# A planned attention and token/channel mixer kernel: all engine orders set anew, last row group in two parts

## The chip, the cores and the metric

The kernel runs on one core of one Trainium2 chip. The metric is device microseconds of one execution. A core has a matmul engine (TensorE, PE in the profile, with its weight loads listed apart as PEld), a vector engine (VectorE, DVE), an activation engine (ScalarE, ACT), a general one (GpSimd, POOL) and a queue engine (SyncE, SP). Each runs its own instructions in the order in which the program lists them, and waits at semaphores for the others. PSUM, where matmuls write, has eight banks.

## The reference

Attention over 4 batches, 8 heads, 768 positions and 64 elements a head, with a mask of blocks (neighbours, first and last rows and columns, and three sampled blocks a row), then a mixer over the 4 x 768 x 512 result:

```python
scores = scale * np.matmul(q, k.transpose(0, 1, 3, 2))      # scale = 1/8
scores = np.where(mask, scores, -1e9)
attn = softmax(scores)                                      # over keys
x = np.matmul(attn, v)             # heads side by side: 4 x 768 x 512
h = np.maximum(xt @ w_tok1, 0.0) @ w_tok2     # xt = x transposed: mixes the 768 positions, 256 hidden
u = x + h.transpose(0, 2, 1)
h2 = np.maximum(u @ w_ch1, 0.0) @ w_ch2       # mixes the 512 channels, 1536 hidden
return u + h2
```

## The kernel before

Two heads make a pair, and there are 16 pairs `p`, four a batch. Each pair has three query tiles `t` of 256, and each of those has three key steps `jj` of 256, so there are 144 steps and 48 units `(p, t)`.

A step is four score matmuls (L917), one exp of 128 x 1024 on ACT (L930) and, in its unit, the product of the probabilities with v (L1086, or L375 for 64-row matmuls). Pairs 0 to 3 (phase 0) carry the mask in 24 extra contraction rows, so their score matmuls have 88 rows. Pairs 4 to 15 (phase 1) use 64-row matmuls, two side by side, and a multiply of the probabilities with a mask on DVE (`cut`, L948), one for the three steps of a unit. `norm` (L1040, L1041) divides by the row sums. K and q are transposed on PE for pairs below 8 (`transposes`, L858 and L823, evacuated at L834, L871 or L887) and by DMA for the others.

When a batch's x is complete, the token mixing follows (`tok_first` for batch 0 pair by pair, `tok_halves` and `tok_full` for the others), then a transpose to `uT`, then the channel mixing `ch`: `uT` with `w_ch1`, relu into `rc`, `rc` with `w_ch2`, an add on DVE (`fin`, L1567 or L1615 and L1622) and the output DMA on SP. The last batch's `ch` has nothing left to mix with. Its last group of 128 rows is written in parts of 256, 128 and 128 columns (L1594).

In `halves` (L365) two 64-row products accumulate in one bank, one pass after the other. Between the passes a no-operation on SP or POOL (`fence`, L358) waits for the first.

The order of every engine is set ahead of time by a planner (`Planner`, L104) that runs while the program is built. It keeps a clock for PE, ACT, DVE and SP and one time `Ev` for each result. An operation has a cost for each engine that may run it, the results it needs, and a priority (the smallest goes first). At each moment a free engine takes the ready operation of the best priority, and its result is dated with the cost, a latency (`lat`) and a semaphore's 50 ns (L283). The order so found is the order in the program; the times are used for nothing else. The priorities and limits are named knobs in `BASE`, overridden by `BY_TIME` for each stretch of planned time (`stretch`). The planner's costs are written beside each operation: `act_cost`, `dve_psum`, 948 for an exp, 1719 for a `cut` over three steps.

Loads are issued on POOL in a fixed order. `landing` dates each as the queue's last landing plus its bytes at 200 B/ns, plus an extra from `LATE` for the first nine, in the order v of pair 0, k, q, v of pair 1, k, q, v of pair 2, and the two token weights.

Of the kernel before, what the change touches and what calls it, by code (L numbers as in the profile page):

```python
# [18 lines left out]
    backp=0.45, backt=0.3, turn=[1], ra=5,  # L19
)  # L20
BY_TIME = {
    0: dict(cch=2),
    1: dict(norm=2.3, m2=300.0, tokp=0.7, ev2=2.0, cch=3),
    2: dict(m2=450.0, ev2=0.9, cpo=1),
    3: dict(norm=2.3, m2=300.0, tokp=0.7, ev2=2.0, cch=3, cpm=3, shift=6000.0, add=0.3, grace=100.0, ev4=1.2),
    5: dict(norm=2.3, m2=150.0, tokp=0.7, ev2=2.0, cch=3, cpm=3, shift=6000.0, add=0.3, grace=100.0, ev4=1.2, cps2=3, relayk=2.0, cut=0.7),
    6: dict(fin=4.1, cps=3, trp=1.6),
    7: dict(fin=4.1, cps=3, trp=1.6),
    8: dict(fin=4.1, cps=3, trp=1.6, add=0.3, back=1.1, cut=0.5),
    9: dict(shift=6000.0),  # L30
    10: dict(fin=4.1, cps=3, trp=1.6, add=0.3, back=1.1, cut=0.5, m2=300.0, ev2=0.9, jit=300.0),
    12: dict(fin=4.1, cps=3, trp=1.6, add=0.3, back=1.1, cut=0.5, m2=300.0, ev2=0.9, jit=300.0, tokp=1.7, backp=0.9, cpo=2, m1=0.0),
    13: dict(fin=4.1, cps=3, trp=1.6, add=0.3, back=1.1, cut=0.5, m2=300.0, ev2=0.9, jit=2000.0, tokp=1.7, backp=0.9, cpo=2, m1=0.0, late=3.5, relayk=0.8),
    14: dict(m2=0.0, cch=2, m1=0.0, cut=6.0, ev4=1.2),
    16: dict(add=0.3, late=1.05, cch=2, ev4=2.0, relayk=3.5),
    17: dict(m1=0.0, back=1.1, add=0.95),
    18: dict(m1=0.0, back=1.1, add=0.95, cut=1.1, m2=300.0, cpo=2),
    19: dict(cps2=3, toks=0.4, jit=300.0, relayv=3.0, relayk=3.5),
    20: dict(m1=0.0, back=1.1, add=0.95, cut=1.1, m2=0.0, cpo=2, toks=-0.5, backp=0.45, cpm=1),
    21: dict(m1=0.0, back=1.1, add=0.95, cut=1.1, m2=0.0, cpo=2, toks=-0.5, backp=0.45, cpm=1),  # L40
    22: dict(m1=100.0, back=1.1, add=0.95, cut=6.0, m2=0.0, cpo=2, toks=-0.5, backp=0.45, cpm=1, relayk=0.8),
    23: dict(m1=100.0, back=1.1, add=0.95, cut=6.0, m2=0.0, cpo=2, toks=-0.5, backp=0.45, cpm=1, relayk=0.8, jit=300.0, cps=3),
    24: dict(m1=100.0, back=1.1, add=0.95, cut=6.0, m2=0.0, cpo=2, toks=-0.5, backp=0.45, cpm=1, relayk=0.8, jit=300.0, cps=3),
    25: dict(jit=450.0, cps2=2, relayv=4.6),
    27: dict(jit=450.0, cps2=2, relayv=4.6, cps=2, backp=0.45, cpo=2, relu=0.85),
    28: dict(jit=450.0, cps2=2, relayv=4.6, cps=2, backp=0.45, cpo=2, relu=0.85),
    29: dict(jit=450.0, cps2=2, relayv=4.6, cps=2, backp=0.45, cpo=2, relu=0.85, toks=0.4, relayk=4.5),
    30: dict(jit=450.0, cps2=2, relayv=4.6, cps=2, backp=0.45, cpo=1, relu=0.85, norm=0.6, cpm=2, backt=0.9),
    31: dict(back=1.1, cpm=1, jit=1300.0),
    32: dict(jit=450.0, cps2=2, relayv=4.6, cps=2, backp=0.45, cpo=1, relu=0.85, norm=1.0, cpm=2, backt=0.9, m1=100.0, shift=0.0),  # L50
    33: dict(tokp=0.7, cps=3, ev4=1.2, shift=-6000.0, cch=2),
    34: dict(chs=0.8, m1=100.0, ev2=1.2, cpo=2, backt=0.2),
    35: dict(jit=0.0, cpo=2, chs=1.1),
}


class Knobs(dict):

    at, by_time, stretch = 0.0, BY_TIME, 5000.0

# [43 lines left out]
class Planner:  # L104
# [108 lines left out]
    def step(self):  # L213
# [36 lines left out]
        for eng in ("act", "dve", "sp"):  # L250
# [3 lines left out]
            best, exp_at = None, 1e18  # L254
# [5 lines left out]
            for o in self.ops:  # L260
# [4 lines left out]
                if eng == "act" and prio > 0 and self.now + cost["act"] > exp_at + KN["grace"]:  # L265
                    continue
# [8 lines left out]
            if best is not None:  # L275
                prio, num, engines, cost, deps, emit, done, lat, tags = chosen
                self.ops.remove(chosen)
                emit(eng)
                c = cost[eng]
                if self.trace is not None:  # L280
                    self.trace.append((self.now, eng, KN[prio] if isinstance(prio, str) else prio, c))
                self.free_at[eng] = self.now + c
                done.t = self.now + c + lat + self.SEM  # L283
                moved = True
# [10 lines left out]
def kernel(  # L295
# [119 lines left out]
    LATE = (0, 0, 600, 200, 400, 0, 0, 1500, 0)  # L415
# [325 lines left out]
    def act_cost(n):  # L741
        return 0.8333 * n + 95.0

    def dve_psum(n, half=1.0):
        return (150.0 + n * half) / 0.96
# [7 lines left out]
    def relayout(p):  # L753
        lays = {}
        for nm in ("k", "q", "v") if p >= NT0 else ("v",):
# [21 lines left out]
            lays[nm + "ev"] = P.op(("dve", "act") if p >= BASE["ra"] else ("dve",), {"dve": 320.0, "act": 735.0}, deps, emit,  # L777
# [5 lines left out]
    def crossbar(p):  # L783

        lays = relayout(p)
        for nm, bufs, there in (("k", ktb, kT_there), ("q", qtb, qT_there)):
# [6 lines left out]
            ev = P.op(("sp",), {"sp": 1300.0}, deps, emit, prio=1, lat=5000.0)  # L793
            there[p, 0], there[p, 1] = ev, ev

    def transposes(p):
# [15 lines left out]
        for nm, bufs, there in (("k", ktb, kT_there), ("q", qtb, qT_there)):  # L812
# [3 lines left out]
            if p >= NT0 and P.phase == 1:  # L816
# [22 lines left out]
                ev = P.op(("dve", "act"), {"dve": 555.0, "act": 740.0}, [last], evac, prio="ev4")  # L839
# [28 lines left out]
            if p >= NT0:  # L868
                def evac(eng, buf=bufs[p % NV], box=box):
# [4 lines left out]
                    ("dve", "act"), {"dve": 555.0, "act": 740.0}, [last], evac, prio="ev4"  # L874
# [5 lines left out]
            for hd in range(2):  # L880
# [8 lines left out]
                ev = P.op(("dve",), {"dve": 550.0}, [last], evac, prio="ev2")  # L889
# [18 lines left out]
    CUTS = (((0,), (1,), (2,)), ((0, 1), (2,)), ((0, 1, 2),), ((0,), (1, 2)))[BASE["cuts"]]  # L908
# [839 lines left out]
```

The softmax here doesn't subtract the row's maximum and nothing guards it: scores larger than these inputs give would overflow.

## Time and profile before

| | us |
|---|---|
| median of 3 runs (lowest, highest) | 245.59 (245.1, 245.77) |
| span of the profiled execution | 243.4 |
| median less span: what lies around it | 2.2 |
| HBM read, written | 26.74 MB, 6.29 MB |
| DMA engines, mean rate over the span | 108 GB/s |

The page gives the time in which each engine was busy, 40 slices of the span, the chain of work that ended last (followed back from the last instruction to what released each one) and the costliest groups of instructions. In a group's line stand the source line, the engine, the operation, what is written and read, the count, the busy time and the mean of one, and after the bar the time for which the engine stood still just before such instructions and what ended that. A windows view gives the busy time of each engine in a stretch, and a timeline the instructions of a stretch in order, neighbours of one kind merged. Ends of matmuls are modelled, starts are recorded. The duration of an ACT or DVE instruction includes some 100 or 80 ns in which the next one already runs: the exp is recorded with 1025 ns, but with work waiting the next begins 921 ns after it.

### The profile page before, as it was taken

How to read it: one execution, taken by the hardware profiler on the slowest of the kernel's cores; microseconds unless marked ns; L12 is line 12 of the kernel's file. 1: busy time of each engine (PE TensorE's matmuls, PEld its weight loads, DVE VectorE, ACT ScalarE, POOL GpSimd, SP SyncE). 2: the span in 40 equal slices, each digit the busy share in tenths (PEclk: the TensorE clock that was granted, in tenths of full speed). 3: DMA queues.
4: the chain of work that ended last, by engine and by line, in shares of the span. 5: the costliest groups of instructions: out<-in, count | busy, mean ns of one | idle time of the engine just before them, and what ended most of it. 6: DMA issues, size and time to landing. Idle time of an engine off the chain costs nothing.

```text
span 243.4 us, 9647 instructions
## 1 busy us (share of the span) xinstructions
PE 237.0 (97%) x4343; PEld 170.9 (70%) x4343; DVE 172.1 (71%) x285; ACT 170.0 (70%) x187; POOL 49.5 (20%) x86
## 2 busy tenths in 40 slices
PE   7999999999999999999999999999999999999994
PEld 3689999767777677867878667677688664565444
DVE  5975987979899889799789788987687535100222
ACT  6889999868797699788778987798658400366000
POOL 8966987357710000000000000000000000000000
PEclk9999999999999999999999999999999999999999
DMA  7999999999993874131207270501030024200132
GB/s 163 166 214 203 209 207 203 206 201 196 201 180 76 132 167 137 38 118 33 40 3 89 46 155 3 154 25 67 3 67 3 5 89 127 112 3 0 43 132 86
DMA packets 39755, 26.17 MB, mean 108 GB/s; under 512 B 21985, under 2 KB 37105, under 8 KB 39713
## 3 DMA queue, kind: packets, MB, share of 16 engines
q0 software_dynamic: 15104, 12.98, 33.9%
q1 hardware_dynamic: 24064, 12.17, 20.4%
q8 instruction: 34, 0.56, 0.9%
q10 hardware_dynamic: 544, 0.39, 0.6%
q14 instruction: 9, 0.07, 0.1%
HBM read 26.74 MB, written 6.29 MB: 136 GB/s over the span
## 4 chain that ended last, share of the span: by engine, by line
PE 89%; DMA 3%; ACT 3%; POOL 2%; DVE 1%; issue 0%; POOLq 0%; DVEq 0%; ACTq 0%
PE banks L375 53%; PE banks L917 14%; PE banks L1601 9%; PE banks L1536 6%; DMA kraw<-in_k_dram 3%; ACT et L930 3%; PE banks L1086 3%; PE banks L858 1%; PE banks L1354 1%; DVE et L948 1%; POOL vraw L447 1%; PE banks L1296 1%; PE banks L1376 1%; PE banks L1318 1%; POOL ktb L517 0%
## 5 line engine op out<-in xcount | busy, mean ns | idle before, releaser
L930 ACT ACTIVATE et<-banks 128x1024 bf16<-128x1024 f32 x144 | 141.6, 1025 | 28.3 <-PE banks L917 24.5
L948 DVE TENSOR_TENSOR et<-et,mask 128x2976 bf16<-128x2976 bf16 x36 | 61.3, 1703 | 8.3 <-ACT et L930 8.2
L917 PE MATMUL banks<-qtb,ktb 64*128 64x256 bf16 (+1 forms) x576 | 63.7, 270 | 0.7 <-ACT et L930 0.2
L375 PE MATMUL banks<-uT,w_ch 64*128 64x512 bf16 (+1 forms) x576 | 60.6, 322 | 0.0
L375 PE MATMUL banks<-w_ch,rc 64*128 64x512 bf16 x384 | 54.3, 376 | 0.0
L375 PEld LDWEIGHTS <-et 64*128 64x128 bf16 x1728 | 39.2, 94 | 9.4 <-POOLq L361 3.0
L917 PEld LDWEIGHTS <-ktb 64*128 64x128 bf16 (+1 forms) x576 | 33.8, 94 | 15.1 <-issue 1.4
L375 PE MATMUL banks<-vaug,et 64*128 64x65 bf16 x1728 | 42.0, 190 | 0.2 <-issue 0.2
L375 PEld LDWEIGHTS <-w_ch 64*128 64x128 bf16 x576 | 28.6, 94 | 8.4 <-SPq L361 0.6
L1128 ACT ACTIVATE rc<-banks 128x512 bf16<-128x512 f32 (+1 forms) x28 | 21.0, 749 | 17.0 <-PE banks L1536 15.0
L1615 DVE TENSOR_TENSOR o<-banks,x 128x512 f32<-128x512 f32 x7 | 4.8, 692 | 28.2 <-PE banks L1601 28.2
L1130 DVE TENSOR_SCALAR rc<-banks 128x1024 bf16<-128x1024 f32 x17 | 20.8, 1221 | 3.4 <-PE banks L375 3.2
L375 PEld LDWEIGHTS <-rc 64*128 64x128 bf16 x384 | 17.3, 94 | 7.9 <-POOLq L361 0.5
L1601 PE MATMUL banks<-w_ch,rc 128*128 128x512 bf16 (+2 forms) x120 | 21.3, 337 | 0.0
L1601 PEld LDWEIGHTS <-rc 128*128 128x128 bf16 x120 | 10.7, 98 | 10.6 <-issue 0.8
L375 PEld LDWEIGHTS <-w_tok 64*128 64x128 bf16 x288 | 14.5, 109 | 3.3 <-POOLq L361 0.6
L1041 DVE TENSOR_TENSOR x<-banks,recip 128x256 bf16<-128x256 f32 x36 | 15.3, 425 | 1.2
L1536 PE MATMUL banks<-uT,w_ch 128*128 128x512 bf16 (+1 forms) x96 | 15.8, 326 | 0.0
L1536 PEld LDWEIGHTS <-w_ch 128*128 128x128 bf16 x96 | 9.4, 98 | 6.4
L1567 DVE TENSOR_TENSOR o<-banks,x 128x1024 f32<-128x1024 f32 x8 | 9.8, 1224 | 5.1 <-PE banks L375 5.0
L1086 PE MATMUL banks<-vaug,et 128*128 128x65 bf16 x288 | 13.1, 193 | 0.0
L1264 DVE TENSOR_TENSOR x<-banks,x 128x512 bf16<-128x512 f32 (+2 forms) x12 | 10.3, 887 | 2.9 <-PE banks L375 2.7
(122 smaller groups left out, 198.0 us busy)
## 6 DMA issues: line engine op xcount, KB each, us to landing
out_dram<-o SPq DMA_DIRECT2D x8, 512.0 KB, 3.6
w_ch<-in_moe_w_ch_dram POOLq DMA_DIRECT2D x8, 384.0 KB, 9.8
vraw<-in_v_dram POOLq DMA_DIRECT2D x10, 192.0 KB, 7.9
out_dram<-o SPq DMA_DIRECT2D x7, 256.0 KB, 2.0
kraw<-in_k_dram POOLq DMA_DIRECT2D x9, 192.0 KB, 9.2
qraw<-in_q_dram POOLq DMA_DIRECT2D x9, 192.0 KB, 8.3
w_tok<-in_moe_w_tok_dram POOLq DMA_DIRECT2D x2, 384.0 KB, 10.0
qf<-in_v_dram POOLq DMA_DIRECT2D x4, 192.0 KB, 7.8
```

The source lines that it names most:

```text
L375: mms.append(nc.tensor.matmul(out=outs()[o](x), lhsT=lhs(o, x, r), rhs=rhs(o, x, r), start=(back == 0 and x == 0), stop=(back == 1 and x = ...
L917: nc.tensor.matmul(out=ps[:, hd, 256 * i : 256 * i + 256], lhsT=ktb[n][rows, h, 256 * jj + 128 * i : 256 * jj + 128 * i + 128], rhs=qtb[n] ...
L930: nc.scalar.activation(out=ets[p, t][:, jj, :, :, :].rearrange("k i h q -> k h i q"), in_=ps.rearrange("k h (i q) -> k h i q", i=2), func= ...
L948: nc.vector.tensor_tensor(out=et, in0=et, in1=free(mask[:, 2 * lo, 256 * t + EDGE : 256 * t + EDGE + 1], 0, [[S, 2 * n], [0, 2], [1, w]]), ...
L1041: nc.vector.tensor_tensor(out=free(xs[b][:, pb // 2, 2 * t, 128 * (pb % 2) : 128 * (pb % 2) + 128], 0, [[64, 2], [256, 2], [1, 64]],), in0 ...
L1086: nc.tensor.matmul(out=po[:, hd, c, :], lhsT=et[:, jj, i, hd, 128 * c : 128 * c + 128], rhs=va[:, hd, 2 * jj + i, 0:65], start=(jj == 0 an ...
L1128: nc.scalar.activation(out=o(), in_=src(), func=AF.Relu)
L1130: nc.vector.tensor_scalar(out=o(), in0=src(), scalar1=0.0, scalar2=None, op0=ALU.max)
L1264: nc.vector.tensor_tensor(out=u, in0=src, in1=u, op=ALU.add)
L1536: nc.tensor.matmul(out=in_bank(pbox["pm"], [k, 128 * n])[:, x // 4, :], lhsT=w_ch1[:, x % 4, 128 * cc : 128 * cc + 128], rhs=st[b]["uT"][: ...
L1567: nc.vector.tensor_tensor(out=t[:, :, :].rearrange("p c (g e) -> p g c e", g=2), in0=free(banks[:, pbox["pm"][0], :], 0, [[256, 2], [512, ...
L1601: nc.tensor.matmul(out=pbox["pm"][:, 0:n], lhsT=box["rc"][:, cc, 128 * sc : 128 * sc + 128], rhs=w_ch2[:, cc, lo : lo + n], start=(cc == 0 ...
```

## The change

The knobs get a value for each 2.5 us of planned time instead of 5; nearly all values are new. The planner's durations, the latency after ACT operations and the extras of the loads are replaced. The mask multiply can be split in a different way for each unit (`cuts=1` is steps 0 and 1 together, then 2; `cuts=0` three single ones; before, `cuts=2` for all). A rule is added by which DVE does not begin an operation of a priority above `urge` that would end later than 200 ns (at `hold=1200`) before one at or below `urge` is ready. Two options, `early` and `part`, are added and are 0. The last row group is written in parts of 384 and 128 columns.

```diff
-    backp=0.45, backt=0.3, turn=[1], ra=5,
+    backp=0.45, backt=0.3, turn=[1], ra=5, early=0, part=0, hold=0.0, urge=-0.5,
...
-BY_TIME = {
-    0: dict(cch=2),
-    1: dict(norm=2.3, m2=300.0, tokp=0.7, ev2=2.0, cch=3),
...
+BY_TIME = {}
+for _lo, _hi, _knobs in (
+    (0, 1, dict(cch=2)),
+    (2, 2, dict(cch=3, ev2=2.0, m2=300.0, norm=2.3, tokp=0.7)),
...
+    (8, 8, dict(backt=0.3, cuts=0, ev4=2, m1=200, relayk=3.5)),
...
+    (18, 19, dict(backt=0.3, cut=1.1, cuts=1, ev4=2, fin=2.1, hold=1200, jit=450, m1=200, m2=450, relayk=3.5, relu=0.85, shift=6000.0)),
...
+    (58, 59, dict(back=1.1, backp=0.45, backt=0.3, cpm=2, cps2=2, cut=1.1, cuts=1, ev2=0.9, ev4=2, fin=2.1, hold=1200, jit=450, m1=200, m2=450, norm=1, relayk=3.5, relayv=4.6, toks=-0.5, urge=0.5)),
...
-    at, by_time, stretch = 0.0, BY_TIME, 5000.0
+    at, by_time, stretch = 0.0, BY_TIME, 2500.0
...
+            if eng == "dve" and KN["hold"] > 0:
+                for o in self.ops:
+                    p = KN[o[0]] if isinstance(o[0], str) else o[0]
+                    if p <= KN["urge"] and "dve" in o[2]:
+                        t = self.when(o[4], o[8])
+                        if t is not None:
+                            soon = min(soon, max(t, self.now))
...
+                if eng == "dve" and prio > KN["urge"] and self.now + cost["dve"] > soon + 1e3 - KN["hold"]:
+                    continue
...
-                done.t = self.now + c + lat + self.SEM
+                done.t = self.now + c + lat + self.SEM + (55.0 if eng == "act" else 0.0)
...
-    LATE = (0, 0, 600, 200, 400, 0, 0, 1500, 0)
+    LATE = (0, 0, 970, 0, 1360, 0, 0, 730, 150)
...
-        return 0.8333 * n + 95.0
+        return 0.8333 * n + 62.0
...
-        return (150.0 + n * half) / 0.96
+        return (100.0 + n * half) / 0.96
...
-                ev = P.op(("dve", "act"), {"dve": 555.0, "act": 740.0}, [last], evac, prio="ev4")
+                ev = P.op(("dve", "act"), {"dve": 500.0, "act": 660.0}, [last], evac, prio="ev4")
...
-    CUTS = (((0,), (1,), (2,)), ((0, 1), (2,)), ((0, 1, 2),), ((0,), (1, 2)))[BASE["cuts"]]
+    CUTS = (((0,), (1,), (2,)), ((0, 1), (2,)), ((0, 1, 2),), ((0,), (1, 2)))
+    cut_of = {}
...
-        exps[jj] = P.op(("act",), {"act": 948.0}, [done], exp, prio=0, lat=80.0)
+        exps[jj] = P.op(("act",), {"act": 915.0}, [done], exp, prio=0)
...
-        for group in CUTS:
+        for group in CUTS[cut_of.setdefault((p, t), KN["cuts"])]:
...
-            ev = P.op(("dve",), {"dve": 158.0 + (537.0 - 4.2 * EDGE) * len(group)},
+            ev = P.op(("dve",), {"dve": 90.0 + 520.0 * len(group)},
...
-            parts[-1:] = [(NC - 1, 0, 256), (NC - 1, 256, 128), (NC - 1, 384, 128)]
+            parts[-1:] = [(NC - 1, 0, 384), (NC - 1, 384, 128)]
...
-                    o = sbw.tile([128, 256], FP32, tag="olast", bufs=3, name=f"o{b}_{sc}_{lo}")
+                    o = sbw.tile([128, 384], FP32, tag="olast", bufs=2, name=f"o{b}_{sc}_{lo}")
...
-                    g, e = lo // 256, lo % 256
-                    nc.vector.tensor_tensor(
-                        out=o[:, 0:n], in0=pbox["pm"][:, 0:n],
-                        in1=st[b]["u"][:, g, sc, e : e + n], op=ALU.add,
-                    )
+                    cuts = sorted({lo, max(lo, min(lo + n, 256)), lo + n})
+                    for l0, l1 in zip(cuts, cuts[1:]):
+                        nc.vector.tensor_tensor(
+                            out=o[:, l0 - lo : l1 - lo], in0=pbox["pm"][:, l0 - lo : l1 - lo],
+                            in1=st[b]["u"][:, l0 // 256, sc, l0 % 256 : l0 % 256 + l1 - l0], op=ALU.add,
+                        )
```

The other operations' planned durations change in the same way (the 768-element copies of a relayout from 320 and 735 to 290 and 660, `norm` from 610 to 570, a DMA transpose's latency from 5000 to 3500 or from 4000 to 3400).

## The prediction

> **What bounds the kernel now.** I read the page's engine shares, slices and chain first, then the windows view stretch by stretch, then the timeline of the stretches where TensorE is not full.
>
> ```profile
> span 243.4 us, 9647 instructions
> ...
> PE 237.0 (97%) x4343; PEld 170.9 (70%) x4343; DVE 172.1 (71%) x285; ACT 170.0 (70%) x187; POOL 49.5 (20%) x86
> ...
> PE   7999999999999999999999999999999999999994
> ...
> PE 89%; DMA 3%; ACT 3%; POOL 2%; DVE 1%; issue 0%; POOLq 0%; DVEq 0%; ACTq 0%
> ...
> L930 ACT ACTIVATE et<-banks 128x1024 bf16<-128x1024 f32 x144 | 141.6, 1025 | 28.3 <-PE banks L917 24.5
> L948 DVE TENSOR_TENSOR et<-et,mask 128x2976 bf16<-128x2976 bf16 x36 | 61.3, 1703 | 8.3 <-ACT et L930 8.2
> ```
>
> The page says TensorE (PE) twice: 97% busy, and 89% of the chain. A busy matmul engine is not proof of a full one, so I checked it with start times. In the last row groups twelve matmuls of 512 columns take 2.59 us, twelve of 256 take 1.31, twelve of 128 take 0.67: 216, 109 and 56 ns each, which is columns/2.4 + 2.5 ns. Two matmuls of 64 rows run side by side, so each counts half. Charged so, all 4343 come to 228.06 us. The first starts at 1.00 and the last is through at 239.94, so PE stands still for 239.94 - 1.00 - 228.06 = 10.88 us. The matmul start times place it: 2.22 before 5.94 us (start-up; the diff does not touch it), 3.05 from 5.94 to 20, 0.22 from 20 to 40, 2.84 from 40 to 55, 1.98 from 55 to 195, 0.57 after. What a new order can win lies in those 8.66 us; after PE's last column come 3.41 us of tail. The windows view (length, then PE, PEld, DVE, ACT, POOL busy with counts, clock, DMA, GB/s) shows the same stretches:
>
> ```profile
> 6.00:20.00 14.00, 13.02 (x187) 10.48 (x185) 11.57 (x29) 12.31 (x14) 11.69 (x20) 1.00 1.17 192
> 40.00:55.00 15.00, 14.33 (x334) 11.07 (x333) 12.78 (x25) 11.86 (x14) 7.80 (x11) 1.00 1.28 204
> 55.00:195.00 140.00, 139.98 (x3128) 103.25 (x3126) 117.41 (x157) 111.01 (x116) 9.35 (x14) 1.00 0.44 84
> 195.00:240.10 45.10, 45.10 (x334) 25.09 (x329) 10.45 (x16) 11.35 (x19) 0.00 (x0) 1.00 0.22 74
> ```
>
> In the long middle PE is full, ACT is at 79% and DVE at 84%: neither binds there, they only have to be on time.
>
> **What the Trainium skill says.** "TensorE: Matmul & The Clock Gate", section Part 3 (The mechanism): matmuls start and end in program order; only weight loads are pulled ahead. The timeline agrees:
>
> ```profile
> 13.49 0.17 PEld L858 LDWEIGHTS <-kraw 128*128 128x128 bf16 x3 [0.71 <-DMA kraw<-in_k_dram]
> 13.49 0.34 PE L858 MATMUL banks<-ident,kraw 128*128 128x128 bf16 x3 [0.54 <-DMA kraw<-in_k_dram]
> ...
> 13.92 0.60 PE L917 MATMUL banks<-qtb,ktb 88*128 88x256 bf16 x4
> ...
> 14.55 1.02 ACT L930 ACTIVATE et<-banks 128x1024 bf16<-128x1024 f32 x1 [0.79 <-PE banks L917]
> ```
>
> Transposes of pair 2's k waited for its DMA, and score matmuls behind them waited too, so ACT ran dry for 0.79 us. "TensorEngine Tiling (Array Packing)", Key Properties: changing the tiling mode drains the array. The trace agrees: 12 changes between full and 64-row matmuls carry 1.16 us of the stalls, mostly 95 ns each. "VectorE: DVE Perf Modes", section on the TRN2 errata: an SBUF-source instruction costs a fixed 58 cycles (60 ns) over its elements. The mask multiply fits: 2976 elements at two a cycle are 1550 ns, its start-to-start time with work waiting is 1616, so 66 fixed.
>
> **The change, part by part.** No PE column is added or removed, except 12 matmuls fewer in the last group (12 x 2.5 ns = 0.03 us). So the new time is the old one plus the change in stalls and tail.
>
> *Landings (LATE).* With 192 KB at 200 B/ns = 0.98 us each, the old plan had pair 1's q at 9.76 us, pair 2's k at 12.33, q 13.31, v 14.30, the two token weights at 17.76 and 19.73. The landing events in the trace are at 10.13, 13.45, 14.41, 15.39, 18.12, 20.23; the new numbers give 10.13, 13.46, 14.44, 15.42, 18.12, 20.24. The planner will no longer queue those transposes 1.1 us early. That wait cost PE 0.70 of the 3.05 us; two score groups at 8.97 and 9.88 lost 0.31 each behind a rescheduled neighbourhood. Gain between 0 (few loads have landed, so nothing else to run) and 1.4; I take 0.8.
>
> *Durations.* Old allowance, new allowance and start-to-start time in the trace: exp 948, 915, 921; mask multiply over three 1719, 1650, 1616; 1024 columns out of PSUM on DVE 1223, 1171, 1141; 768-column evacuation on DVE 555, 500, about 470. The latency added after an ACT operation rises from 80 to 115 (60 to 115 for others). Alone this moves nothing; it makes the greedy planner pick what really is ready.
>
> *Mask multiply in two parts* (cuts=1 nearly everywhere that pair 4 and later are planned; the cuts=0 of 20 to 25 us is never used, since their first scores start at 41.77). DVE gets some 36 more instructions, at 66 ns (fit above) to 158 (the old constant): 2.4 to 5.7 us. In 55 to 195 DVE has 140 - 117.4 = 22.6 us idle, which hides it; without that cover the end would move by the whole. In return the probability-value product need not wait for a 1703 ns multiply after its last exp: the last part is estimated at 583. That shows at the seam, where everything waits for the first multiply:
>
> ```profile
> 45.60 0.26 PE L823 MATMUL banks<-ident,qlay 64*128 64x64 bf16 x6
> 46.09 0.39 PE L917 MATMUL banks<-qtb,ktb 64*128 64x256 bf16 x4 [0.23 <-ACT et L930]
> 46.37 1.41 PE L375 MATMUL banks<-a_t,w_tok 64*128 64x128 bf16 x20
> ```
>
> Stalls of 0.40 (46.09), 0.28 and 0.30 (inside the 20 matmuls) and 0.36 (53.55) make 1.34 of the seam's 2.84; 0.67 is mode changes, which alternating kinds of work needs. I take 1.2 won, bounds -0.5 and 2.0.
>
> *hold/urge.* DVE may now stay idle for an urgent operation. Until 145 us `urge` is -0.5 but for one 2.5 us step, so only pair 3's first token step qualifies; later the token adds do. DVE idles then, on cover. early=0 and part=0 leave those two edits without effect.
>
> *Knobs.* Every order in 55 to 195 is new. There are 1.98 us of stalls, mostly crumbs under 60 ns. Bounds +4 and -1.2; I take 0.3 won.
>
> *Last row group in two parts.* SP's queue after DVE:
>
> ```profile
> 237.49 0.69 DVE L1615 TENSOR_TENSOR o<-banks,x 128x512 f32<-128x512 f32 x1 [1.90 <-PE banks L1601]
> 238.21 2.58 SPq L1626 DMA_DIRECT2D out_dram<-o  x4
> 238.80 0.42 DVE L1622 TENSOR_TENSOR o<-banks,x 128x256 f32<-128x256 f32 x1 [0.62 <-PE banks L1601]
> 239.47 0.29 DVE L1622 TENSOR_TENSOR o<-banks,x 128x128 f32<-128x128 f32 x1 [0.25 <-PE banks L1601]
> 240.14 0.29 DVE L1622 TENSOR_TENSOR o<-banks,x 128x128 f32<-128x128 f32 x1 [0.38 <-PE banks L1601]
> ```
>
> The 384 columns finish at 239.44; their two adds (0.34 to the next start, then 0.29) end at 240.07, one issue on SP takes 0.33, until 240.43. The last add ends at 240.40, so its DMA goes out where it did, at 240.46, up to 0.05 later. But 192 KB instead of 64 KB stand ahead of it; 256 KB took 0.8 us of packets, so they need 0.6 and may push the last packets from 241.65 to 241.95. Cost 0 to 0.35, taken as 0.15; 128 KB used to leave 0.8 us earlier, and that cover is gone.
>
> Sum: -0.8 - 1.2 - 0.3 + 0.15 = -2.15 us. The span 243.35 becomes 241.2. The median of the runs, 245.59, stands 2.24 above the span (what lies around it); carried over, 243.4 us.
>
> **Rivals.**
> *Stalls only move* (within 0.3%, which is 0.74 us and about what a measurement here can tell from no change): the start has nothing else to run, since ACT is the bound right after (busy 19.89 of the 20 us from 20 to 40), and the seam's waits come back one operation later. For it: PE is already 97% filled from 20 us on (5.61 us of stalls in 220). Against: four waits of about 0.3 us or more at the seam have a named cause. 245.6.
> *The slack was the cover* (slower). The old allowances exceeded the trace by 27 ns an exp and 103 a multiply; the new ones by -6 and 34. In an in-order PE queue an operation planned exactly on time waits whenever ACT or DVE runs a little late, and two extra semaphore steps a unit add chances. Place: the 34 units between 55 and 195 us. At 120 ns a unit it costs 4.1 us; less the 1.85 won elsewhere and in the tail, +2.2: 247.8. It decides from (1.85 + 0.74)/34 = 76 ns a unit on. For it: of the 24.2 us that ACT idles in this stretch, 20.7 end with a score matmul, so the two are tightly meshed. Against: ACT is 21% idle there and two score banks are buffered.
> *The seam closes entirely*: start 1.4, seam 2.0, middle 0.8 won, tail 0.15 lost: 241.5. For it: lighter multiplies and known landings. Against: mode changes cannot vanish.
>
> **How the numbers follow.** Forecast 0.55, stalls only move 0.10, slower 0.22, seam closes 0.13. The forecast's own range, from half to one and a half times its sum, is 242.4 to 244.5. The range reaches down past 241.5 to 241.0 and up to 247.2, through part of the slower case. Faster 0.68, same 0.10, slower 0.22.
>
> **What would show it.** Right: PE stalls from 5.94 to 20 near 2.2, from 40 to 55 near 1.6, the middle at or below 2; no transposes of kraw waiting near 13.5; 72 mask multiplies in place of 36, DVE under 90% in the middle. Wrong: middle stalls over 4 us with PE waiting for ACT or the multiply; a tail over 3.8 us; or weights (w_ch) or pairs landing later because their buffers come free later.

## The result, and the profile after

The changed kernel takes 244.5 us (median of 20 runs, 244.16 to 247.33), and the kernel before, run beside it, 244.82 (20 runs, 244.24 to 245.77): a ratio of 0.999, 95% interval 0.9974 to 1.0006. That is no change that this measurement can tell, where 243.4 against 245.59 was forecast. The three runs that the forecast started from lay high: 20 give 0.8 us less for the same kernel.

The page of the changed kernel, with the lines that answer to those shown of before (L974 is the exp, L992 the mask multiply):

```profile
span 243.1 us, 9668 instructions
...
PE 237.6 (98%) x4337; PEld 172.4 (71%) x4337; DVE 173.1 (71%) x314; ACT 174.5 (72%) x192; POOL 49.8 (20%) x86
...
PE   8899999999999999999999999999999999999995
...
PE 93%; ACT 3%; DMA 2%; SPq 0%; issue 0%; DVE 0%
...
L974 ACT ACTIVATE et<-banks 128x1024 bf16<-128x1024 f32 x144 | 142.7, 1025 | 27.8 <-PE banks L961 25.9
L992 DVE TENSOR_TENSOR et<-et,mask 128x1984 bf16<-128x1984 bf16 (+2 forms) x70 | 65.3, 951 | 5.4 <-ACT et L974 4.9
```

The multiply did become 70 instructions instead of 36, of 951 ns in the mean instead of 1703, at a cost of 4.0 us of recorded DVE time. PE looks fuller, 98% and 93% of the chain. Its span is 0.2 us shorter. Busy shares say nothing at this size, so here are the stretches by windows (length, then PE, PEld, DVE, ACT, POOL busy with counts, clock, DMA, GB/s):

```profile
6.00:20.00 14.00, 12.78 (x186) 10.31 (x184) 11.71 (x30) 12.94 (x15) 11.60 (x20) 1.00 1.18 193
40.00:55.00 15.00, 14.81 (x337) 10.84 (x337) 12.20 (x22) 12.79 (x15) 8.03 (x12) 1.00 1.28 204
55.00:195.00 140.00, 139.96 (x3120) 105.41 (x3118) 119.17 (x188) 114.21 (x118) 9.28 (x13) 1.00 0.47 84
195.00:240.10 45.10, 45.10 (x324) 24.72 (x320) 11.11 (x18) 11.43 (x20) 0.00 (x0) 1.00 0.22 74
```

At the seam (40 to 55) PE's busy time rises from 14.33 to 14.81, which looks like half a microsecond won. It is not: busy time includes the modelled end of each matmul and hides stalls shorter than that. The stalls, counted as in the prediction from start times, with those at a change between full-height and 64-row matmuls shown apart, are (us):

| | span | PE through | tail | 5.94–20 | 20–40 | 40–55: waits + changes | 55–195 | 195–205 |
|---|---|---|---|---|---|---|---|---|
| before | 243.35 | 239.94 | 3.41 | 3.05 | 0.22 | 2.17 + 0.67 (7 changes) | 1.98 | 0.57 |
| after | 243.12 | 239.94 | 3.19 | 3.07 | 0.21 | 1.47 + 1.51 (15) | 2.24 | 0.36 |

Stalls are 0.19 us more, the matmuls themselves 0.19 less (one group of q's transposes is done in 64-row halves, side by side), so PE is through at the same 239.94. The 0.21 us won from 195 to 205 (three changes of shape instead of five) is lost again at the seam and in the middle, so all that the span won is in the tail. The profiled execution took 244.85, 1.7 more than its span.

The seam in the timeline of the changed kernel, PE alone (start, length, engine, line, operation, shape, count):

```profile
45.60 0.22 PE L418 MATMUL banks<-vaug,et 64*128 64x65 bf16 x4
45.75 0.37 PE L1422 MATMUL banks<-a_t,w_tok 128*128 128x128 bf16 x3
46.05 0.43 PE L418 MATMUL banks<-a_t,w_tok 64*128 64x128 bf16 x8
46.41 0.26 PE L1422 MATMUL banks<-a_t,w_tok 128*128 128x128 bf16 x1
46.60 0.32 PE L418 MATMUL banks<-a_t,w_tok 64*128 64x128 bf16 x4
...
47.56 0.35 PE L866 MATMUL banks<-ident,klay 64*128 64x64 bf16 x12
47.91 0.80 PE L1451 MATMUL banks<-ident,x 64*128 64x64 bf16 x24
48.80 0.35 PE L866 MATMUL banks<-ident,qlay 64*128 64x64 bf16 x12
```

The scores that waited 0.40 us for an exp at 46.09 in the kernel before are gone from here. In their place PE does three token products of 128 rows, goes back to 64, does one of 128, and goes back again: four changes in one microsecond, about 100 ns each. Three stalls of some 170 to 270 ns between 47.9 and 48.8 are new as well.

The start, in the same view:

```profile
5.94 0.70 PE L961 MATMUL banks<-qtb,ktb 88*128 88x256 bf16 x4
7.42 0.28 PE L628 MATMUL banks<-ident,qlay_first 128*128 128x128 bf16 x2 [0.79 <-ACT qlay_first L620]
7.64 0.27 PE L643 MATMUL banks<-ktb,t2add 24*24 24x256 bf16 x1
...
12.43 0.60 PE L961 MATMUL banks<-qtb,ktb 88*128 88x256 bf16 x4
12.87 0.89 PE L1130 MATMUL banks<-vaug,et 128*128 128x65 bf16 x24
13.60 0.60 PE L961 MATMUL banks<-qtb,ktb 88*128 88x256 bf16 x4
```

No transposes of pair 2's k wait at 13.5 any more. But PE now waits 0.8 us at 7.42 for a copy whose input, the last half of pair 0's q, landed at 6.73 us; in the profile of before it landed at 5.42. Neither that load, nor its place in its queue, nor its time of issue (1.78 and 1.79) is touched by the change.

### The profile page after: what moved, and what is told of

It reads as the page before. It is cut to its first block, busy times and chain, and to the rows that moved or that the text cites. A ratio compares the mean times of both kernels' runs of the same rounds, so it can differ in the third digit from the quotient of the medians.

```text
span 243.1 us, 9668 instructions
## 1 busy us (share of the span) xinstructions
PE 237.6 (98%) x4337; PEld 172.4 (71%) x4337; DVE 173.1 (71%) x314; ACT 174.5 (72%) x192; POOL 49.8 (20%) x86
## 3 DMA queue, kind: packets, MB, share of 16 engines
HBM read 26.74 MB, written 6.29 MB: 136 GB/s over the span
## 4 chain that ended last, share of the span: by engine, by line
PE 93%; ACT 3%; DMA 2%; SPq 0%; issue 0%; DVE 0%
PE banks L418 54%; PE banks L961 15%; PE banks L1648 9%; PE banks L1583 6%; PE banks L1130 3%; ACT et L974 2%; DMA qf<-in_q_dram 2%; PE banks L901 1%; PE banks L1422 1%; PE banks L1400 1%; PE banks L1340 1%; PE banks L1362 1%; PE banks L866 0%; ACT ktb L877 0%; PE banks L1481 0%; ACT qlay_first L620 0%
## 5 line engine op out<-in xcount | busy, mean ns | idle before, releaser
L974 ACT ACTIVATE et<-banks 128x1024 bf16<-128x1024 f32 x144 | 142.7, 1025 | 27.8 <-PE banks L961 25.9
L992 DVE TENSOR_TENSOR et<-et,mask 128x1984 bf16<-128x1984 bf16 (+2 forms) x70 | 65.3, 951 | 5.4 <-ACT et L974 4.9
L418 PE MATMUL banks<-w_ch,rc 64*128 64x512 bf16 x384 | 56.5, 376 | 0.0
L418 PEld LDWEIGHTS <-et 64*128 64x128 bf16 x1728 | 41.4, 94 | 8.6 <-POOLq L404 1.9
L961 PEld LDWEIGHTS <-ktb 64*128 64x128 bf16 (+1 forms) x576 | 35.2, 94 | 15.2 <-issue 1.9
L418 PE MATMUL banks<-vaug,et 64*128 64x65 bf16 x1728 | 44.7, 190 | 0.0
L418 PEld LDWEIGHTS <-w_ch 64*128 64x128 bf16 x576 | 26.9, 94 | 9.2 <-POOLq L404 0.7
L1172 ACT ACTIVATE rc<-banks 128x512 bf16<-128x512 f32 (+1 forms) x26 | 18.9, 727 | 14.1 <-PE banks L1583 14.1
L1174 DVE TENSOR_SCALAR rc<-banks 128x1024 bf16<-128x1024 f32 x19 | 23.1, 1219 | 0.9 <-PE banks L418 0.8
L418 PEld LDWEIGHTS <-rc 64*128 64x128 bf16 x384 | 18.8, 94 | 6.1 <-issue 0.4
L1084 DVE RECIPROCAL recip<-banks 128x4 f32<-128x4 f32 x36 | 6.5, 179 | 10.1 <-PE banks L418 10.1
```

What stands on the lines that cost most here:

```text
L418: mms.append(nc.tensor.matmul(out=outs()[o](x), lhsT=lhs(o, x, r), rhs=rhs(o, x, r), start=(back == 0 and x == 0), stop=(back == 1 and x = ...
L961: nc.tensor.matmul(out=ps[:, hd, 256 * i : 256 * i + 256], lhsT=ktb[n][rows, h, 256 * jj + 128 * i : 256 * jj + 128 * i + 128], rhs=qtb[n] ...
L974: nc.scalar.activation(out=ets[p, t][:, jj, :, :, :].rearrange("k i h q -> k h i q"), in_=ps.rearrange("k h (i q) -> k h i q", i=2), func= ...
L992: nc.vector.tensor_tensor(out=et, in0=et, in1=free(mask[:, 2 * lo, 256 * t + EDGE : 256 * t + EDGE + 1], 0, [[S, 2 * n], [0, 2], [1, w]]), ...
L1084: nc.vector.reciprocal(out=recip[:, :, :], in_=free(po, 64, [[512, 2], [65, 2]]))
L1172: nc.scalar.activation(out=o(), in_=src(), func=AF.Relu)
```

## The experiments

The four theories: **A, landings**: the start differs with when loads happen to land, not with the order. **B, one budget**: at the seam the planner trades waits for changes of shape, and the sum stays. **C, planned waits**: the middle's gain was planned waiting time that the chip never had. **D, cover** (the prediction's slower rival): DVE, with more instructions and tighter plans, is late. Most edits below keep the order of every engine as planned and change one thing inside it, for one knob more or less replans all that follows. Times are medians, and ratios are to the kernel before, run beside each.

### Pair 2's k earlier, in the kernel before

Pair 1's v is asked for after pair 2's k; the planned order is as it was.

```diff
+            issue = lambda out=raw, src=src: nc.gpsimd.dma_start(
...
+            if (nm, p) == ("v", 1):
+                held.append(issue)
+            else:
+                issue()
+            if (nm, p) == ("k", 2):
+                held.pop()()
```

> The kernel before, order of all engines as it was; only pair 2's k is issued ahead of pair 1's v, so that it should land about 1 us earlier (near 12.4 instead of 13.45 us) and v about 1 us later (near 12, needed at 12.7). Landing theory (the new order's gain at the start is no more than not waiting for this load in executions where it lands late): the wait before the k transposes near 13.5 goes, the stall of TensorE from 5.94 to 20 us falls from 3.05 to about 2.4, and the median falls by 0.3 to 0.6 us, to that of the changed kernel. Rival (other work was ready behind it anyway, or the start isn't what sets the end): within 0.2 us of before.

244.89 us, ratio 0.9984 (0.9972 to 0.9995). Pair 2's k lands at 11.20, and the timeline at the place of the old wait is:

```profile
13.20 0.60 PE L925 MATMUL banks<-qtb,ktb 88*128 88x256 bf16 x4
13.64 0.65 PE L1094 MATMUL banks<-vaug,et 128*128 128x65 bf16 x16
14.12 0.27 PE L925 MATMUL banks<-qtb,ktb 88*128 88x256 bf16 x1
```

The wait is gone, the stalls from 5.94 to 20 fall from 3.05 to 2.36, and every later stretch is as before to 0.1 us (middle 1.98 again). So a wait at the start is worth its full length at the end of the profiled span (242.55), but the medians differ by only 0.2%. That fits a wait which not every execution has.

### Two parts in the kernel before, three in the changed one

The diff of the last group, put into the kernel before; and taken out of the changed kernel.

```diff
-            parts[-1:] = [(NC - 1, 0, 256), (NC - 1, 256, 128), (NC - 1, 384, 128)]
+            parts[-1:] = [(NC - 1, 0, 384), (NC - 1, 384, 128)]
```

> The kernel before with the last row group in parts of 384 and 128 columns, nothing else. My forecast's step: 0.15 us slower, up to 0.35. What the trace of the changed kernel suggests: about 0.2 us faster, since its end waits for all DMAs in a list, 61 ns for each entry, and the last DMA stood third in that list before and near its end now.

> The changed kernel with the last row group in three parts as before, all else as changed. If the tail in two parts is worth 0.2 us, this is 0.2 us above the changed kernel, that is about equal to before; by my forecast's step it would be 0.15 us below it.

Two parts in the kernel before: 244.79 us, 0.9981 (0.9971 to 0.999); three in the changed one: 244.74, 0.9985 (0.9975 to 0.9996). In the profiles the tail is 3.19 us with two parts and 3.39 with three, whatever the order. The sign is opposite to the prediction's. What SP waits for at the end tells why, in the waits view of SP (line, waited for, us in total, times, longest), first of the kernel before:

```profile
SPq L1743 <- DMA out_dram<-o: 1.1, 1, 1.1
```

and of the changed kernel:

```profile
SPq L1791 <- DMA out_dram<-o: 0.7, 2, 0.6
```

Before the program ends, SP goes through a list of waits, one for each DMA semaphore in use, some 61 ns each. In the kernel before the last output stood third in it: the wait ended at 242.01 and seven more entries followed. With two parts it stands last: the list is gone through while the transfer runs, and ends with it at 242.21, although the last packets, as the prediction said, are later (by 0.2 us, 241.85 against 241.65).

In these two kernels the start differs too, unasked: pair 2's k lands at 12.51 and 11.82, and the start's stalls are 2.64 and 2.57. The 0.70 us wait for it, from which the prediction's first step was worked out, is not there in the kernel before with two parts, where nothing at the start was edited. Yet up to 20 us that profile has as many stalls as the one of before, 5.27 us, because it has 2.63 instead of 2.22 before 5.94: PE reached its full pace later (see the part on the start below).

### The mask multiply in two parts, alone

In the kernel before, each multiply is issued as two, at the same place.

```diff
+                for lo, n in ((0, 2), (2, 1)):
...
-                             [[S, 2 * n], [0, 2], [1, w]]),
+                                 [[S, 2 * n], [0, 2], [1, w]]),
```

> The kernel before, order as it was, with each mask multiply over three steps issued as two instructions in the same place (steps 0 and 1, then 2). Cover theory: VectorE takes 36 x 66 = 2.4 us more and TensorE hides it: within 0.2 us of before. Rival (VectorE's time is what the middle waits for): 0.5 us or more slower.

245.53 us, 1.0011 (0.9992 to 1.0029): nothing that can be told. The middle's stalls are 1.97. Its start has 3.22 us of stalls, with the last half of q landing at 7.16. The seam's are 3.1, not less than the 2.84 before. This edit tests only the added instructions; the part that a product need not wait for was not tried alone.

### Half of each mask multiply left out

`[[512, 2 * n]` becomes `[[1024, n]` in both kernels, so each instruction does half the elements, and the rest stays unmasked. It takes some 24 to 27 us of work off DVE and leaves every order.

> The changed kernel with every mask multiply over half of its columns (every second block of 128 keys), order unchanged; the other half of the mask is not applied for pairs 4 to 15. It takes about 28 us off VectorE. Slack theory (my rival: with tighter durations TensorE waits for VectorE running late, which ate the gain): 0.5 to 0.9 us faster than the changed kernel, and stalls of the middle (55 to 195 us) fall from 2.2 to under 1.5. Paper theory (the waits that the new durations removed in the middle existed only in the plan): within 0.3 us of the changed kernel, middle stalls 1.9 to 2.2.

> The kernel before with every mask multiply over half of its columns, order unchanged, half of the mask not applied for pairs 4 to 15. Both theories: middle stalls stay near 2.0. The seam (40 to 55 us), where TensorE waits after the first multiplies, shows what the length of a multiply costs there: seam stalls from 2.84 to 2.3 to 2.6, so 0.2 to 0.5 us faster than before; if over 1 us faster, the multiplies' length was what the middle paid for.

The changed kernel with thin multiplies: 244.56 us, 0.9979 (0.9969 to 0.9989); the kernel before: 245.09, 1.001 (1.0001 to 1.002). The middle's stalls are 2.62 and 2.33 us, above the 2.24 and 1.98 with whole multiplies, and above what either theory expected. Were PE waiting in the middle for a DVE that is late, a DVE at 61% would have ended it. D falls, as far as it speaks of DVE and the multiplies; ACT that runs late was not tested.

The seam is the test of the prediction's largest step. In the kernel before with thin multiplies it has 2.89 us of stalls, where 2.3 to 2.6 was expected and 2.84 stood before. DVE in the timeline of before:

```profile
45.22 1.71 DVE L948 TENSOR_TENSOR et<-et,mask 128x2976 bf16<-128x2976 bf16 x1 [0.20 <-ACT et L930]
46.85 0.55 DVE L1385 TENSOR_TENSOR x<-banks,x 128x384 bf16<-128x384 f32 x1
```

and DVE and PE with the thin multiply:

```profile
44.74 0.93 DVE L948 TENSOR_TENSOR et<-et,mask 128x1488 bf16<-128x1488 bf16 x1 [0.37 <-ACT et L930]
45.59 0.55 DVE L1385 TENSOR_TENSOR x<-banks,x 128x384 bf16<-128x384 f32 x1
45.60 0.40 PE L917 MATMUL banks<-qtb,ktb 64*128 64x256 bf16 x4 [0.23 <-ACT et L930]
...
47.11 0.48 PE L375 MATMUL banks<-vaug,et 64*128 64x65 bf16 x20 [0.17 <-ACT et L930]
```

Of the four waits that the prediction named, one hung on the multiply: the 0.30 us for the add at L1385, which stood behind the multiply on DVE. It is gone, and PE waits 0.34 us for an exp at 47.11 instead, one operation later. The 0.40 us for an exp stands (now at 45.60), and so do the other two.

### Both small gains, and pair 2's k earlier in the changed kernel

> The kernel before with two edits that leave the order of its engines as it was: pair 2's k issued ahead of pair 1's v, and the last row group in two parts. If both gains stand and add, 0.9984 x 0.9981 = 0.9965 of before, so some 0.8 us faster, and at or below the changed kernel (0.999). If one was noise, 0.998 to 0.999.

> The changed kernel with pair 2's k issued ahead of pair 1's v. Its order does not wait for that k, so by the landing theory nothing changes: within 0.2 us of the changed kernel. If it gains 0.4 us or more, the new order waits for loads at the start as well, and the landings it was given are not those of most executions.

The kernel before with both edits: 244.71, 0.9989 (0.9979 to 0.9999). The two gains do not add: their product would be 0.9965. The changed kernel with k earlier: 244.61, 0.9985 (0.9973 to 0.9997). In the latter the start's stalls fall by 0.74 to 2.33, but the middle's rise from 2.24 to 2.80. Its timeline shows one of the places (in brackets: idle before, and what ended it):

```profile
97.73 0.83 ACT L816 COPY qlay<-ktb 128x768 bf16<-128x768 bf16 x1 [0.30 <-DMA qtb<-qlay]
...
98.47 0.59 ACT L1270 ACTIVATE a_t<-banks 128x512 bf16<-128x512 f32 x1
...
99.11 0.64 PE L418 MATMUL banks<-a_t,w_tok 64*128 64x256 bf16 x8 [0.21 <-ACT a_t L1270]
```

A copy into `qlay` waits for the DMA transpose that still reads it, the relu behind it on ACT is late, and the token product stalls 0.39 us. The change shortened that transpose's planned latency from 5000 to 3500 ns, so with the 1300 ns of its issue the plan gives it 4.8 us where it gave 6.3. It took 5.39 us from issue (92.19) to landing, and 5.23, 4.50 and 5.13 us in three other profiles of the changed order, where the copy came later than the landing. So here the new allowance is shorter than the chip. Whether the old one would have avoided the wait was not tried; the edited kernel differs from the changed one only in two early loads.

### Fewer changes of shape

Knobs were drawn anew by plan alone for an order with 12 changes instead of 18, at the same planned end. Only values in `BY_TIME` differ, and a term by which an operation of the other shape can be put back:

```diff
+                turn = s[3] and not callable(s[3]) and s[3][5] != self.mode
+                order.append((prio + (KN["pen"] if turn else 0.0), s[1], s, prio))
```

> The changed kernel with knobs drawn anew so that the order has 12 changes of the tile's shape in place of 18 (9 in place of 15 at the seam of 40 to 55 us), at the same planned end (238.56 us against 238.63). The plan itself has more waits at the seam for it (1.73 against 1.17 us), and the middle as in the changed kernel (0.83 against 0.84). Theory, changes and waits are one budget: the seam's stalls are again 2.8 to 3.2 us, changes 0.9 and waits 2.0 to 2.3, and the span is within 0.3 us of the changed kernel's 243.1; median 244.3 to 244.8. Rival, the six added changes were what ate the seam's gain: the waits stay at the 1.5 us of the changed kernel, the seam's stalls fall to about 2.4 us, span 242.6, and the time is 0.2 to 0.3% below the changed kernel's.

> The kernel with 12 changes of shape, and in it pair 2's k asked for before pair 1's v as well. If a landing between 10.6 and 11.2 us is worth what it was in the kernel before (0.69 us in its start) and the seam's gain stands, it is the fastest of all: span 242.1, median 243.9 to 244.3. If, as in the changed kernel with that one edit, what is won at the start is lost again later (0.74 won, 0.56 lost in the middle), the span is 242.8 to 243.3 and the median within 0.3 us of the changed kernel's.

245.13 us, 1.0019 (0.9998 to 1.0041); with k earlier 244.83, 1.0003 (0.999 to 1.0017). Neither beats the changed kernel. At the seam the changes cost 1.01 us instead of 1.51, and the waits 1.87 instead of 1.47: 2.88 in sum, against 2.98 and 2.84 in the changed kernel and the one before. The PE timeline shows a wait where a change was:

```profile
46.97 0.32 PE L423 MATMUL banks<-a_t,w_tok 64*128 64x128 bf16 x4
47.08 0.24 PE L423 MATMUL banks<-vaug,et 64*128 64x65 bf16 x2
47.38 0.32 PE L423 MATMUL banks<-a_t,w_tok 64*128 64x128 bf16 x4
...
49.39 0.32 PE L871 MATMUL banks<-ident,qlay 64*128 64x64 bf16 x10 [0.32 <-ACT ktb L882]
```

Between 47.08 and 47.38 stands a stall of 240 ns, and one of 486 before 49.39. That is B as expected. The order was chosen for the same planned end, so an equal sum at the seam was built into its plan; what the run adds is that the chip follows the plan there. The start was 3.30 us in the first of the two (q's last half at 6.29) and 3.55 in the second (at 6.88), where 2.3 was hoped for from k being early: A.

### Only the old landings, in the changed kernel

```diff
-    LATE = (0, 0, 970, 0, 1360, 0, 0, 730, 150)
+    LATE = (0, 0, 600, 200, 400, 0, 0, 1500, 0)
```

> The changed kernel with the old planned landings only: its knobs, which count by planned time, then fall on other work, and the planned end is 246.2 us, 7.6 later, 5.5 of it planned waits of the PE between 55 and 195 us, with 26 changes of shape. Theory, the plan's waits are real where they are long and only its small ones are not on the chip: the middle's stalls rise from 2.2 to between 5 and 8 us, and the time is 2 to 3% above the kernel before's. Rival, the plan's clock has little to do with the chip's: the middle's stalls stay under 3.5 us and the time is within 1%.

252.45 us, 1.0305 (1.0282 to 1.0328), 7.95 above the changed kernel, where the plan said 7.6. The middle's stalls are 7.27. The exps in the stretch from 55 to 195 us (a group as on the page, with more than one releaser):

```profile
L974 ACT ACTIVATE et<-banks 128x1024 bf16<-128x1024 f32 x96 | 96.6, 1024 | 31.2 <-PE banks L961 30.0 <-PE banks L418 0.5
```

Only 96 exps fit into the stretch, where the changed kernel has 100. This is not what the landings are worth: the knobs count by planned time and fall on other work. It shows that the planner's clock is good to some 2 us in 250 (0.5 to 2.0 in the table below), and that the parts of this change cannot be undone one by one through the planner.

### The last half of q earlier

In the changed kernel with k earlier, the load of the sampled blocks (0.6 KB) is issued last on SP instead of first.

```diff
-    nc.sync.dma_start(out=samp64[R, :], in_=sampled_blocks)
...
     first(nc.sync, "q", q, 1)
+    nc.sync.dma_start(out=samp64[R, :], in_=sampled_blocks)
```

> The changed kernel with pair 2's k before pair 1's v, and the small load of the sampled blocks issued last on SP instead of first, so that SP's halves of k and q for pair 0 are issued 0.45 us earlier (0.81 and 1.27 in place of 1.31 and 1.78). Theory, what differs between executions at the start is when the last half of q and pair 2's k land: that half lands by 5.0 to 6.0, no wait of 0.9 us at 7.4 to 7.9, stalls from 5.94 to 20 us 2.0 to 2.4, span 242.3 to 242.9, median 244.1 to 244.4, with a spread below the changed kernel's. Against it: the sampled blocks then land at about 3.3 us, DVE's mask of the blocks is 0.4 us later, and with it ACT's copy at 4.09 and all that follows it on ACT, so the start loses 0.3 to 0.5 and the median is 244.7 to 245.0. A third outcome, that half of q waits for its share of the DMA engines and not for its issue: it lands between 5.2 and 7.2 as before, and the time is that of the kernel with k first, 244.6.

249.52 us (247.36 to 251.2, 6 runs), 1.0158 (1.0113 to 1.0203) without the longest of them. The half of q lands at 5.18, as the theory says. But the timeline of the start shows what it cost:

```profile
1.83 0.48 SPq L545 DMA_DIRECT2D samp<-in_sampled_blocks_dram  x1
...
5.68 0.23 DVE L614 TENSOR_TENSOR differ<-kbi,samp 24x72 f32<-24x72 int32 x1 [2.86 <-DMA samp<-in_sampled_blocks_dram]
...
6.42 0.28 PE L651 MATMUL banks<-ktb,t2add 24*24 24x256 bf16 x1 [2.68 <-DVE t2add L621]
```

Issued first, at 0.81, the small load was there when DVE wanted it at 2.74. Issued 1 us later it was not there until 5.68: it stood behind the 192 KB loads. I had priced the delay at 0.3 to 0.5 us. PE stands still for 3.1 us before that one matmul, which starts 2.75 us later than in the kernel with k early (6.42 against 3.67), and the lowest run is 2.3 us above the kernel before. The profile is of the longest execution, 251.2 us, and its windows show a second loss (clock: the third number from the end):

```profile
10.00:15.00 5.00, 5.00 (x28) 3.16 (x27) 3.07 (x8) 3.44 (x4) 3.81 (x6) 0.50 1.22 200
```

The granted TensorE clock is 0.50 from 7.3 to 21.0 us, where the windows of before and after shown above have 1.00, and four score matmuls of 256 columns take 1.06 us there instead of 0.60. How the other five executions, with clocks of 0.999 or 1.0 on record and no trace, come to lie between 247.4 and 250.8 stays open, and so does why the clock fell.

## Why the prediction was wrong

The sum said -2.15 us; the span moved by -0.23 and the medians by -0.32. Its terms, as the prediction put them:

| step | predicted | profile of after against before | what the runs showed |
|---|---|---|---|
| landings, start | -0.8 | +0.02 | one execution's landings |
| multiply in two parts, seam | -1.2 | +0.14 | waits -0.70, changes +0.84 |
| knobs, middle | -0.3 | +0.26 | planned waits that were not on the chip |
| last group in two parts | +0.15 | -0.22 | SP's list of waits |

**The step that failed most is the seam's, -1.2 us.** The prediction has everything there wait for the first multiply, counts four waits (0.40, 0.28, 0.30, 0.36) as nearly all won, and keeps the 0.67 us of changes as fixed, "which alternating kinds of work needs". Both halves were wrong. Only one of the four hung on the multiply, as the thin multiply shows: half the length leaves 2.89 us of stalls at the seam. In the line that the prediction quotes for the longest, what ended the wait is an exp. The changed order does fill the four waits, but with work of the other shape, 15 changes instead of 7, and with new waits of its own: waits fall by 0.70 and changes rise by 0.84. The fewer-changes order gave the opposite trade and the same sum. "TensorEngine Tiling (Array Packing)", Key Properties, says that a change drains the array; it gives no price. Here it is 96 to 112 ns in the mean: 0.67 us for 7, 1.51 for 15, 1.01 for 9.

**The new plan was there to be read.** The planner charges 98 ns for a change (L227), and building the two kernels gives its waits without the chip: 1.73 and 1.76 us up to 20 us, 1.98 and 1.17 at the seam (with the changes 2.67 and 2.64), 1.26 and 0.84 in the middle, and a last matmul 0.84 us earlier. The prediction took 2.0 us from the start and the seam, where the new plan itself wins nothing. It asked which stalls of the old order could go, not which order the changed kernel has.

**The start's step took one draw for a rule.** `LATE` was set to the landings in a trace, and the prediction compared it with the same profile, where it fits to 0.05 us. Pair 2's k, at 13.45 there, landed at 12.51, 13.88 and 12.96 in three further profiles with the same early loads, and at 12.72, 11.82 and 12.38 in three with the changed order. The start's stalls were 3.05, 2.64, 3.22 and 2.36 (mean 2.82) in the first four, 3.07, 2.57 and 2.65 (mean 2.76) in the others. With four against three profiles a gain of 0.1 or 0.2 can be neither seen nor excluded; one of 0.8 would show. A second draw is the last half of q: in the four profiles where it landed at 6.29 or later, PE stands still for 0.6 to 1.1 us before the transposes that need it. A third is PE's pace. Four matmuls of 256 columns take 0.61 us at 4.11 in the profile of before and 1.06 at 4.17 in that of after, and the last one at half pace starts anywhere from 2.7 to 6.8 us in these seven. So the stalls before 5.94, which the prediction set aside as untouched, are 2.22 to 2.63. Counted from the first matmul to 20 us the means are 5.26 and 5.07.

**The middle.** The planner's own clock has PE waiting in each stretch too. Beside the chip (waits without changes, us):

| kernel | seam: planned, chip | middle: planned, chip | last matmul: planned (with the 0.23 us until its result is there), chip |
|---|---|---|---|
| before | 1.98, 2.17 | 1.26, 1.98 | 239.47, 239.94 |
| after | 1.17, 1.47 | 0.84, 2.24 | 238.63, 239.94 |
| fewer changes | 1.73, 1.87 | 0.83, 2.30 | 238.56, 240.52 |
| old landings | 2.09, 2.32 | 6.35, 7.27 | 246.21, 247.46 |

At the seam the chip follows the plan to 0.3 us, and where the plan waits long, in the last row, it does so in the middle. But the 0.4 us that the plan of the changed kernel wins in the middle is not there: the kernel before had 1.97 to 1.99 in five profiles (2.33 with thin multiplies), mostly stalls below 60 ns that no plan has, and the changed order, with shorter allowances, 2.03 to 2.80. At the last matmul the chip is later against the changed plan by 0.84 us more than against the old one, which is what the plan had won. Most of this comes about in the middle: from the seam on the kernel before stays 0.6 to 0.8 us behind its plan, and the changed one falls from 0.8 to 1.5 behind by 153 us.

Place by place one sees why. The old plan's three longest single waits there, 0.27 us near 175, 0.15 near 93 and 0.11 near 114, are about 0.19, 0.06 and 0.08 on the chip. The changed plan's two longest, 0.17 near 126 and 0.12 near 57, are about 0.18 and 0.15, each for an exp. So part of what the old plan waits is not on the chip, as its longer allowances would have it, and leaving that out wins nothing. Then there are waits in no plan that differ between executions of the changed order: 0.20 us near 60 in its profile and none with the last group in three parts, 0.39 at 99.1 with k early. C fits all of this. It was not isolated by a run of its own: an order with the old allowances and the same seam can't be had from the planner.

**The rival that came true** is "stalls only move", given 0.10. Its reason at the start (ACT binds right after) was not the one found; its words on the seam, that waits come back one operation later, are what the thin multiply showed. "The slack was the cover" asked for 76 ns a unit in 34 units; the middle's stalls grew by 8 ns a unit, and lighter multiplies took none away. A piece of it came true elsewhere, at the DMA transposes whose allowance was cut: 0.39 us, in one profile.

**The tail.** The prediction had the end follow the last packets. They did come 0.2 us later, but the end follows SP's list of waits, which it left out, and that is through 0.2 us earlier.

**The base.** 2.24 us around the span mixed one profile's span with a median of other runs. In the changed kernel and in the experiments, an execution takes 1.64 to 1.77 us more than its own span. That error has the other sign: with 1.7 the forecast would have been 242.9, and further off.

What is left of a gain is small: the changed order's kernels with a ratio (0.999, 0.9985, 0.9985) and the single edits of the old one (0.9984, 0.9981) all lie at 0.1 to 0.2%. The single edits together gave 0.9989, so differences of this size are not to be added up. The lowest run of the two kernels, 244.16 and 244.24, is nearly the same time.

## What to carry to other kernels

When an engine is 97% full, a better plan wins only what the chip really waits: split its stalls into waits, changes of shape and crumbs, ask of each wait what really ended it, and of each filled wait which changes the filling brings. Where the new order is known before it runs, read what it claims to win stretch by stretch. Never tune planned arrival times to one trace; take several profiles of the same program and plan for their spread, or issue the load earlier. And a plan chosen because it is short is short partly through its own errors: compare plan and chip stretch by stretch before a planned gain below the plan's own error (here 0.5 to 2 us) is believed.

## What was not expected of the hardware

- Loads of one program land up to 2 us apart from one execution to the next: pair 2's k at 11.82 to 13.88 us, the last half of q at 5.19 to 7.16, with their issues at equal times.
- A load of 0.6 KB, asked for behind 192 KB loads, was not there until 3.85 us after its issue began; ahead of them it took at most 1.93.
- The order in which SP waits for finished DMAs at the end of the program is worth 0.2 us: each entry after the last landing takes 61 ns.
- The time from which PE runs at full pace differs between executions of one program: the last matmul at half pace starts from 2.7 to 6.8 us. In one execution with a wait of 3.1 us at the start the clock was 0.50 again from 7.3 to 21.0 us.
